# Attention, a rational layer and a routed layer on one core: softmax scaling, an affine step and a weight conversion recast

## The chip, the cores and the metric

The kernel runs on one core of a Trainium2 chip. The metric is the device time of one execution in microseconds; the median of three runs is given. A core has a matrix engine (PE, whose weight loads are listed as PEld), a vector engine (DVE), a scalar engine (ACT, or ScalarE), GpSimd (POOL) and a queue that starts transfers (SP).

## The reference

Three layers follow one another, on 4 x 576 = 2304 tokens of 512 features.

```python
# attention, 8 heads of 64, causal window of 128, ALiBi bias
scores = np.where(mask, scale * q @ k.T + bias, -1e9)
attn = np.exp(scores - scores.max(-1, keepdims=True))
attn = attn / (attn.sum(-1, keepdims=True) + 1e-9)
x = attn @ v
# rational layer, 512 -> 2048 -> 512
h = x @ w_in
P = a[0] + a[1]*h + a[2]*h**2 + a[3]*h**3
Q = 1 + abs(b[0])*abs(h) + abs(b[1])*h**2
y = (P / (Q + 1e-6)) @ w_out
# routed layer: 8 experts, 512 -> 1024 -> 512, one expert a token
e = argmax(y @ w_gate)
out = softmax(y @ w_gate)[e] * (relu(y @ w1[e]) @ w2[e])
```

The weights of the rational layer come as float64 numbers.

## The kernel before

**Stage A** takes the 2304 tokens in 9 chunks of 256. For each chunk it runs the rational layer in 8 steps; a step multiplies two 128-column slices of `w_in` (`up`, L366 to L368), turns the result `h_ps` into `P/Q` (`rational`, L380 to L415), and two steps later multiplies by the matching rows of `w_out` (`down`, L375 to L377). Each number is carried as two float32r parts, so that three products stand for one. Beside the steps of chunk c runs the attention of chunk c+1: four pairs of heads, one yield of `attention` for every second step. **Stage B** then runs the chosen experts in chunks of 256 tokens, with weights that are loaded and split on the way (`load_split`).

**Attention of a pair of heads.** A chunk of 256 tokens falls into two or three tiles of up to 128 rows, because 576 is no multiple of 256. For a tile and its two heads r = 0, 1: scores on PE (L290 or L299), bias and maximum on DVE (L304, with an accumulator read behind it), exponential and row sum on ACT (L309), 1e-9 added to the two sums (L313), reciprocal (L316), the division by the sum (L327 on DVE, in chunk 0 L325 on ACT, in chunk 1 L319 on POOL), the transposes on PE (L336), the copy to SBUF on ACT (L341, or L344 where the two blocks of keys differ in rows), and P.V on PE (L347), which writes head 0 to the output partitions 0 to 63 and head 1 to 64 to 127:

```python
for r in range(2):
    for i, (_, n, vb) in enumerate(blocks):
        nc.tensor.matmul(x_ps[D*r:D*r+D, qcol:qcol+L], v_sb[0:n, vb, D*r:D*r+D],
                         pt_sb[0:n, r, i, 0:L], start=(i == 0), stop=(i == nb - 1))
```

There are 80 such pairs of heads and tiles: 8 in chunk 0, 8 in chunk 1, 64 in chunks 2 to 8. In 16 of them one block of keys has 128 rows and the other 64. A float32 matmul stands in the trace as two instructions.

**Rational layer of a step** (tiles of 128 x 512): `ah` = |h| on ACT (L387), `u` = a3 h + a2 on ACT (L388), `qq` = |b1||h| + |b0| on DVE (L394; in chunk 0 on ACT, L390), `qq` times `ah` on POOL (L397), logarithm and exponential on ACT (L398, L399) for the reciprocal, five products on DVE (L400 to L410), the rounded part on ACT (L413) and the rest of it on POOL (L414).

**Conversion of the float64 weights** (`fetch64`, `magnitude64`, `split64`), in chunk 0: 16 tiles, each in two halves of 128 x 512. A half is one Abs on ACT (L170), four DVE instructions (clamp L171, shift L180, two steps that join bits, L183 and L186), one rounding on ACT (L189) and one subtraction on POOL (L190). The first 14 tiles (`EARLY`) lie whole in slots of the ring of weights and are handled as two views; the last two come as two tiles each.

**Order of the work.** The kernel is written with tiles; a scheduler that simulates the engines sets the order of each engine's instructions when the program is built (`schedule_with_timeline_sim=True`). On the chip each engine takes its instructions in that order.

Of the kernel before, what the change touches and what calls it, by code (L numbers as in the profile page):

```python
# [22 lines left out]
P = 128  # L23
T = 256
RING = 16               # resident weight tiles
RAWB = 2
EARLY = 14              # float64 tiles staged in the slots of the weights to come
AH1, AH2 = 2, 1         # how far the loads and the magnitudes run ahead of the splits
LEAD0, LEADR, LEAD = 0, 1, 4
PACK = 2                # from this chunk on, q and k are split into float32r parts  # L30
ACTN, POOLN = (0,), (1,)  # chunks whose softmax is divided by its sum on ScalarE, on GpSimd
QQA = (0,)              # chunks whose denominators start on ScalarE
POOLLO = (1, 4, 7)      # weight tiles of an expert whose lower parts GpSimd computes
JP, JT = 0, 1           # steps of a chunk at which the next one is gathered and transposed
JP0, JT0, JE = 2, 3, 2

# The upper words of the float64 numbers 2^-127 and of the greatest one below 2^128, read as float32.
# [5 lines left out]
def attention_rational_moe_kernel(  # L43
# [89 lines left out]

    yd = dram.tile([NT + 1, DM], F32, name="yd")
# [15 lines left out]
    def fetch64(f):  # L150
        src = wpack[f].bitcast(I32)
        if f < EARLY:
            raw = ring.tile([P, 2, DM, 2], I32, name="raw64", tag="ring")
            nc.sync.dma_start(out=raw.rearrange("p h n t -> p (h n t)"), in_=src)
            raws[f] = [raw[:, i] for i in range(2)]
# [7 lines left out]
    def magnitude64(f):  # L163
        if f < EARLY:
            a = ring.tile([P, 2, DM], F32, name="mag", tag="ring")
            mags[f] = [a[:, i] for i in range(2)]
        else:
            mags[f] = [ahp.tile([P, DM], F32, name="mag", tag="ah") for _ in range(2)]
        for i, (raw, a) in enumerate(zip(raws[f], mags[f])):
# [5 lines left out]
    def split64(f):  # L175
        w = ring.tile([P, 2, 2 * DM], F32R, name="w", tag="ring")
        for i, (raw, a) in enumerate(zip(raws.pop(f), mags.pop(f))):
            cs = slice(i * DM, (i + 1) * DM)
# [80 lines left out]
    def attention(c, xh, xl):  # L259
        for hp in range(H // 2):  # L260
# [6 lines left out]
            # Rows 0..63 and 64..127 hold both parts of q against the same part of k, so that two  # L267
            # products of the full height give all four terms of a head.
# [14 lines left out]
            for L, qcol, k0, wn, bo, blocks in tiles:  # L283
# [3 lines left out]
                su = sm.tile([P, 2], F32, name="su")  # L287
# [15 lines left out]
                for r in range(2):  # L303
# [7 lines left out]
                        bias=nm[0:L, r:r + 1], accum_out=su[0:L, r:r + 1],  # L311
                    )
                nc.vector.tensor_scalar(  # L313
                    out=su[0:L], in0=su[0:L], scalar1=1e-9, scalar2=None, op0=ALU.add
                )
                nc.vector.reciprocal(out=su[0:L], in_=su[0:L])  # L316
                for r in range(2):
                    if c in POOLN:
                        nc.gpsimd.tensor_scalar(  # L319
                            out=p_sb[0:L, r, 0:wn], in0=p_sb[0:L, r, 0:wn],  # L320
                            scalar1=su[0:L, r:r + 1], scalar2=None, op0=ALU.mult,
                        )
                        continue
                    if c in ACTN:
                        nc.scalar.mul(p_sb[0:L, r, 0:wn], p_sb[0:L, r, 0:wn], su[0:L, r:r + 1])  # L325
                        continue
                    nc.vector.tensor_scalar(  # L327
                        out=p_sb[0:L, r, 0:wn], in0=p_sb[0:L, r, 0:wn],
                        scalar1=su[0:L, r:r + 1], scalar2=None, op0=ALU.mult,
                    )  # L330
# [433 lines left out]
```

## Time and profile before

| | us |
|---|---|
| median of 3 runs (lowest, highest) | 960.73 (960.16, 961.38) |
| span of the profiled execution | 957.6 |
| PE busy | 857.6 (90%) |
| PEld busy | 731.5 (76%) |
| DVE busy | 762.1 (80%) |
| ACT busy | 573.2 (60%) |
| POOL busy | 507.1 (53%) |

The span runs from the first to the last instruction of the profiled execution; its whole time is not given apart, so the median of the runs, which lies 3.1 us above that span, stands for it. An engine's busy share is a mean over stages with different limits, and matmuls overlap in the profile, so that a busy PE is not PE at its peak. The start-to-start distance of two instructions on an engine tells more of what one costs than its duration.

### The profile page before, as it was taken

The page shows a single profiled execution, that of the slowest core. Times are in us where ns is not written, and L with a number is a line of the kernel's source. Part 1 is how long each engine was busy: PE and PEld are TensorE (multiplying, and loading weights), DVE is VectorE, ACT ScalarE, POOL GpSimd, SP SyncE. Part 2 cuts the span into 40 slices and gives each one's busy share as a digit, 9 for nine tenths or more (in the row PEclk, how much of TensorE's full clock was granted, in tenths as well). Part 3 has the DMA queues.
Part 4 walks back from the last instruction along what each step waited for, and adds up shares of the span by engine and source line. Part 5 has one row for each costly group of instructions (what it writes and reads, how often), then busy time and mean ns, then how long its engine had stood idle before and what let it go on. Part 6 is the DMA issues. An engine that isn't in the chain of part 4 may idle for free. (4 is left out here: it accounts for less than half of the span.)

```text
span 957.6 us, 16505 instructions
## 1 busy us (share of the span) xinstructions
PE 857.6 (90%) x5550; PEld 731.5 (76%) x5550; DVE 762.1 (80%) x1601; ACT 573.2 (60%) x1250; POOL 507.1 (53%) x433
## 2 busy tenths in 40 slices
PE   4557888998999899899899999999998989999994
PEld 2236577887988778778778778788778979999993
DVE  8999989897998998997998998969767875555510
ACT  5767676666676567666566676655536755555510
POOL 7457885453544554544444445435547855555500
PEclk9998899998999999999999999999999999999997
DMA  8553021022123122212112113000149976667400
GB/s 309 206 180 120 33 71 50 31 65 72 48 55 96 34 57 76 58 42 67 37 54 65 52 46 92 10 23 1 56 153 319 319 265 221 221 224 256 148 6 19
DMA packets 69962, 101.89 MB, mean 106 GB/s; under 512 B 14706, under 2 KB 47346, under 8 KB 68083
## 3 DMA queue, kind: packets, MB, share of 16 engines
q1 hardware_dynamic: 64658, 86.11, 28.0%
q0 software_dynamic: 5216, 14.70, 4.4%
q8 instruction: 45, 0.74, 0.3%
q14 instruction: 43, 0.34, 0.1%
HBM read 91.13 MB, written 10.17 MB: 106 GB/s over the span
## 5 line engine op out<-in xcount | busy, mean ns | idle before, releaser
L366 PE MATMUL h_ps<-x,w 128*128 128x256 f32 x896 | 263.9, 297 | 24.8 <-DVE u L401 10.9
L367 PE MATMUL h_ps<-x,w 128*128 128x256 f32 x896 | 262.5, 293 | 7.6 <-DVE x L354 4.2
L368 PE MATMUL h_ps<-x,w 128*128 128x256 f32 x896 | 261.5, 292 | 0.7 <-POOL w L210 0.5
L366 PEld LDWEIGHTS h_ps<-x,w 128*128 128x128 f32 x896 | 176.5, 198 | 36.1 <-issue 16.2
L367 PEld LDWEIGHTS h_ps<-x,w 128*128 128x128 f32 x896 | 177.3, 198 | 13.7 <-DVE x L354 5.3
L375 PE MATMUL y_ps<-w,gh 128*128 128x512 f32 x448 | 180.8, 404 | 3.9 <-ACT gh L413 2.7
L368 PEld LDWEIGHTS h_ps<-x,w 128*128 128x128 f32 x896 | 177.3, 198 | 2.7 <-POOL w L210 1.0
L376 PE MATMUL y_ps<-w,gh 128*128 128x512 f32 x448 | 178.8, 399 | 0.0
L377 PE MATMUL y_ps<-w,gl 128*128 128x512 f32 x448 | 169.5, 400 | 1.0 <-POOL gl L414 1.0
L397 POOL TENSOR_TENSOR qq<-qq,ah 128x512 f32<-128x512 f32 x72 | 98.8, 1373 | 102.1 <-DVE qq L394 78.6
L414 POOL TENSOR_TENSOR gl<-u,gh 128x512 fp32r<-128x512 f32 x72 | 98.7, 1372 | 98.1 <-ACT gh L413 73.5
L210 POOL TENSOR_TENSOR w<-rawh,w 128x512 fp32r<-128x512 f32 x60 | 87.8, 1484 | 49.1 <-ACT w L209 48.7
L309 ACT ACTIVATE p_sb<-p_sb,nm 128x256 f32<-128x256 f32 (+4 forms) x160 | 75.0, 470 | 52.1 <-DVE nm L304 49.3
L377 PEld LDWEIGHTS y_ps<-w,gl 128*128 128x128 f32 x448 | 85.2, 190 | 21.4 <-POOL gl L414 3.7
L375 PEld LDWEIGHTS y_ps<-w,gh 128*128 128x128 f32 x448 | 85.6, 191 | 20.6 <-ACT gh L413 4.5
L376 PEld LDWEIGHTS y_ps<-w,gh 128*128 128x128 f32 x448 | 85.8, 192 | 14.6 <-issue 0.3
L278 POOL TENSOR_TENSOR qk<-k_sb,qk 128x384 fp32r<-128x384 f32 (+1 forms) x56 | 63.7, 1145 | 46.4 <-ACT qk L274 37.7
L413 ACT CAST gh<-u 128x512 fp32r<-128x512 f32 x72 | 44.6, 619 | 54.9 <-DVE u L410 54.5
L347 PE MATMUL x_ps<-pt_sb,v_sb 128*64 128x128 f32 (+3 forms) x576 | 60.9, 294 | 10.6 <-ACT pt_sb L341 8.2
L190 POOL TENSOR_TENSOR w<-mag,w 128x512 fp32r<-128x512 f32 x32 | 51.7, 1632 | 30.3 <-ACT w L189 30.2
L398 ACT ACTIVATE r<-qq,qc 128x512 f32<-128x512 f32 x72 | 51.9, 722 | 26.2 <-POOL qq L397 26.2
L404 DVE SCALAR_TENSOR_TENSOR u<-u,co,r 128x512 f32<-128x512 f32 x72 | 59.3, 823 | 10.3 <-ACT r L399 10.2
(141 smaller groups left out, 1694.9 us busy)
## 6 DMA issues: line engine op xcount, KB each, us to landing
rawh<-epack SPq DMA_DIRECT2D x100, 256.0 KB, 5.3
raw<-epack SPq DMA_DIRECT2D x30, 512.0 KB, 5.6
raw<-wpack SPq DMA_DIRECT2D x14, 1024.0 KB, 7.1
v_sb<-vv SPq DMA_DIRECT2D x92, 64.0 KB, 2.0
k_sb<-kT SPq DMA_DIRECT2D x28, 192.0 KB, 3.6
q_sb<-qT SPq DMA_DIRECT2D x40, 128.0 KB, 2.8
yd<-y_sb POOLq DMA_DIRECT2D x18, 256.0 KB, 2.8
k_sb<-kT SPq DMA_DIRECT2D x16, 160.0 KB, 3.1
```

The source lines that it names most:

```text
L210: (nc.gpsimd if i in POOLLO else nc.vector).tensor_tensor(out=w[:, 1, cs], in0=raw, in1=w[:, 0, cs].bitcast(F32), op=ALU.subtract)
L278: nc.gpsimd.tensor_tensor(out=kl, in0=k_sb[:, r, 0:kc], in1=kh.bitcast(F32), op=ALU.subtract)
L309: nc.scalar.activation(out=p_sb[0:L, r, 0:wn], in_=p_sb[0:L, r, 0:wn], func=AF.Exp, scale=-1.0, bias=nm[0:L, r:r + 1], accum_out=su[0:L, r ...
L347: nc.tensor.matmul(x_ps[D * r:D * r + D, qcol:qcol + L], v_sb[0:n, vb, D * r:D * r + D], pt_sb[0:n, r, i, 0:L], start=(i == 0), stop=(i == ...
L366: nc.tensor.matmul(out_ps, w[:, 0, ws], xh[:, k, :], start=(k == 0), stop=False)
L367: nc.tensor.matmul(out_ps, w[:, 0, ws], xl[:, k, :], start=False, stop=False)
L368: nc.tensor.matmul(out_ps, w[:, 1, ws], xh[:, k, :], start=False, stop=(k == KD - 1))
L375: nc.tensor.matmul(y_ps[t], gh[:, i, ts], w[:, 0, DM:], start=a, stop=False)
L376: nc.tensor.matmul(y_ps[t], gh[:, i, ts], w[:, 1, DM:], start=False, stop=False)
L377: nc.tensor.matmul(y_ps[t], gl[:, i, ts], w[:, 0, DM:], start=False, stop=z)
L397: nc.gpsimd.tensor_tensor(out=qq, in0=qq, in1=ah, op=ALU.mult)
L414: nc.gpsimd.tensor_tensor(out=gl, in0=u, in1=gh.bitcast(F32), op=ALU.subtract)
```

## The change

Five edits. The affine step of every chunk goes to ACT. The sums of a pair lie in one of three constant tiles whose second column holds 1e-9, and one reduction over the two columns takes the place of the addition. Outside chunk 0 the division of both heads is one product of two tensors on DVE, in which the reciprocals are broadcast along the keys; POOL has no share in it any more. The first 14 float64 tiles are converted whole. In P.V the loop over blocks is the outer one.

```diff
+    sums = [const.tile([P, 2, 2], F32, name=f"sum{i}") for i in range(3)]
+    n_sums = [0]
+    for su in sums:
+        nc.vector.memset(su, 1e-9)
...
         if f < EARLY:
-            raw = ring.tile([P, 2, DM, 2], I32, name="raw64", tag="ring")
-            nc.sync.dma_start(out=raw.rearrange("p h n t -> p (h n t)"), in_=src)
-            raws[f] = [raw[:, i] for i in range(2)]
+            raw = ring.tile([P, 2 * DM, 2], I32, name="raw64", tag="ring")
+            nc.sync.dma_start(out=raw.rearrange("p n t -> p (n t)"), in_=src)
+            raws[f] = [raw]
...
         if f < EARLY:
-            a = ring.tile([P, 2, DM], F32, name="mag", tag="ring")
-            mags[f] = [a[:, i] for i in range(2)]
+            mags[f] = [ring.tile([P, 2 * DM], F32, name="mag", tag="ring")]
...
-                su = sm.tile([P, 2], F32, name="su")
+                su = sums[n_sums[0] % len(sums)]
+                n_sums[0] += 1
+                ri = sm.tile([P, 2], F32, name="ri")
...
-                        bias=nm[0:L, r:r + 1], accum_out=su[0:L, r:r + 1],
+                        bias=nm[0:L, r:r + 1], accum_out=su[0:L, r, 0:1],
                     )
-                nc.vector.tensor_scalar(
-                    out=su[0:L], in0=su[0:L], scalar1=1e-9, scalar2=None, op0=ALU.add
-                )
-                nc.vector.reciprocal(out=su[0:L], in_=su[0:L])
-                for r in range(2):
-                    if c in POOLN:
-                        nc.gpsimd.tensor_scalar(
-                            out=p_sb[0:L, r, 0:wn], in0=p_sb[0:L, r, 0:wn],
-                            scalar1=su[0:L, r:r + 1], scalar2=None, op0=ALU.mult,
-                        )
-                        continue
-                    if c in ACTN:
-                        nc.scalar.mul(p_sb[0:L, r, 0:wn], p_sb[0:L, r, 0:wn], su[0:L, r:r + 1])
-                        continue
-                    nc.vector.tensor_scalar(
-                        out=p_sb[0:L, r, 0:wn], in0=p_sb[0:L, r, 0:wn],
-                        scalar1=su[0:L, r:r + 1], scalar2=None, op0=ALU.mult,
+                nc.vector.tensor_reduce(out=ri[0:L], in_=su[0:L], op=ALU.add, axis=AX.X)
+                nc.vector.reciprocal(out=ri[0:L], in_=ri[0:L])
+                if c in ACTN:
+                    for r in range(2):
+                        nc.scalar.mul(p_sb[0:L, r, 0:wn], p_sb[0:L, r, 0:wn], ri[0:L, r:r + 1])
+                else:
+                    nc.vector.tensor_tensor(
+                        out=p_sb[0:L, :, 0:wn], in0=p_sb[0:L, :, 0:wn],
+                        in1=ri[0:L].unsqueeze(2).to_broadcast([L, 2, wn]), op=ALU.mult,
                     )
...
-                for r in range(2):
-                    for i, (_, n, vb) in enumerate(blocks):
+                for i, (_, n, vb) in enumerate(blocks):
+                    for r in range(2):
...
-        if c in QQA:
-            nc.scalar.activation(
-                out=qq, in_=ah, func=AF.Identity, scale=babs[:, 1:2], bias=babs[:, 0:1]
-            )
-        else:
-            nc.vector.tensor_scalar(
-                out=qq, in0=ah, scalar1=babs[:, 1:2], scalar2=babs[:, 0:1], op0=ALU.mult, op1=ALU.add
-            )
+        nc.scalar.activation(
+            out=qq, in_=ah, func=AF.Identity, scale=babs[:, 1:2], bias=babs[:, 0:1]
+        )
```

The scheduler sets the order anew on every engine. Three places follow.

DVE at the conversion of the first two weight tiles (`mag`, `raw`), before:

```order
L171 TENSOR_SCALAR mag<-mag 128x512
L180 TENSOR_SCALAR mag<-mag 128x512
L171 TENSOR_SCALAR mag<-mag 128x512
L183 SCALAR_TENSOR_TENSOR mag<-raw_286,mag 128x512
L180 TENSOR_SCALAR mag<-mag 128x512
L186 SCALAR_TENSOR_TENSOR mag<-raw_286,mag 128x512
L183 SCALAR_TENSOR_TENSOR mag<-raw_286,mag 128x512
L171 TENSOR_SCALAR mag<-mag 128x512 x2
L186 SCALAR_TENSOR_TENSOR mag<-raw_286,mag 128x512
```

and now:

```order
L175 TENSOR_SCALAR mag<-mag 128x1024
L186 TENSOR_SCALAR mag<-mag 128x1024
L189 SCALAR_TENSOR_TENSOR mag<-raw_292,mag 128x1024
L175 TENSOR_SCALAR mag<-mag 128x1024
L192 SCALAR_TENSOR_TENSOR mag<-raw_292,mag 128x1024
```

The four instructions of a tile stand once in place of twice, with twice the columns.

DVE in the middle of stage A, where the softmax of a pair (`su`, now `sum` and `ri`; `p_sb`) stands among the products of the rational layer (`u`, `qq`), before:

```order
L313 TENSOR_SCALAR su<-su 128x2
L354 TENSOR_TENSOR x<-x_ps,x 128x256
L401 SCALAR_TENSOR_TENSOR u<-u,co,h_ps 128x512
L316 RECIPROCAL su<-su 128x2
L327 TENSOR_SCALAR p_sb<-p_sb,su 128x256 x2
L404 SCALAR_TENSOR_TENSOR u<-u,co,r_4531 128x512
L407 SCALAR_TENSOR_TENSOR qq<-qq,qc,r_4531 128x512
L410 SCALAR_TENSOR_TENSOR u<-qq,u 128x512
L394 TENSOR_SCALAR qq<-ah,babs 128x512
```

and now:

```order
L321 TENSOR_REDUCE ri<-sum_189 128x2
L396 SCALAR_TENSOR_TENSOR u<-u,co,h_ps 128x512
L322 RECIPROCAL ri<-ri 128x2
L327 TENSOR_TENSOR p_sb<-p_sb,ri 128x512
L312 ISA p_sb,nm<-s_ps,bm 128x256
L312 ISA nm 128x1
L312 ISA p_sb,nm<-s_ps,bm 128x256
L312 ISA nm 128x1
L399 SCALAR_TENSOR_TENSOR u<-u,co,r_4532 128x512
```

Two products have become one, the addition a reduction, and the affine step has left DVE.

ACT at the same place, a step of the rational layer (`ah`, `u`, `qq`, `r`, `gh`), before:

```order
L387 ACTIVATE ah<-h_ps 128x512
L388 ACTIVATE u<-h_ps,co 128x512
L413 CAST gh<-u 128x512
L309 ACTIVATE p_sb,su<-p_sb,nm 128x256
L398 ACTIVATE r_4666<-qq,qc 128x512
L341 COPY pt_sb<-pt_ps 128x512
L399 ACTIVATE r_4666<-r_4666 128x512
```

and now:

```order
L388 ACTIVATE u<-h_ps,co 128x512
L317 ACTIVATE p_sb,sum_190<-p_sb,nm 128x256
L389 ACTIVATE qq<-ah,babs 128x512
L317 ACTIVATE p_sb,sum_190<-p_sb,nm 128x256
L341 COPY pt_sb<-pt_ps 128x512
L408 CAST gh<-u 128x512
L393 ACTIVATE r_4588<-qq,qc 128x512
```

The affine step stands in ACT's queue ahead of the copy of the transposed tile.

## Rows read from the trace of the kernel before

**Rows 1.** Busy time by stretch: PE, PEld, DVE, ACT, POOL, clock, DMA.

```profile
core 0: us, PE busy (x) PEld busy (x) DVE busy (x) ACT busy (x) POOL busy (x), PEclk, DMA share, GB/s
0.00:130.00 130.00, 84.32 (x417) 59.33 (x418) 125.67 (x275) 86.58 (x200) 90.48 (x103) 0.95 0.47 166
130.00:690.00 560.00, 527.07 (x3580) 450.86 (x3579) 494.70 (x1153) 359.82 (x848) 277.51 (x227) 0.98 0.19 51
```

**Rows 2.** PE's waits, 140 to 690 us: total us, times, longest.

```profile
PE pt_ps L336 <- DVE p_sb L327: 8.4, 12, 1.8
...
PE y_ps L375 <- ACT gh L413: 2.3, 3, 0.9
...
PE h_ps L366 <- DVE oh L461: 1.5, 2, 0.8
```

**Rows 3.** DVE groups by form, 0 to 130 us: count, busy us, mean ns, idle before.

```profile
L183 DVE SCALAR_TENSOR_TENSOR mag<-raw,mag 128x512 int32<-128x512 int32 x31 | 26.0, 856 | 0.0
L180 DVE TENSOR_SCALAR mag<-mag 128x512 int32<-128x512 int32 x31 | 24.3, 804 | 0.1
L186 DVE SCALAR_TENSOR_TENSOR mag<-raw,mag 128x512 int32<-128x512 int32 x31 | 23.4, 768 | 0.0
L171 DVE TENSOR_SCALAR mag<-mag 128x512 f32<-128x512 f32 x32 | 19.5, 626 | 1.2 <-ACT mag L170 1.2
```

**Rows 4.** DVE in order of time, 42 to 52 us: start us, length us.

```profile
42.95 1.28 DVE L183 SCALAR_TENSOR_TENSOR mag<-raw,mag 128x512 int32<-128x512 int32 x2
...
50.70 0.41 DVE L180 TENSOR_SCALAR mag<-mag 128x512 int32<-128x512 int32 x1
51.03 0.68 DVE L183 SCALAR_TENSOR_TENSOR mag<-raw,mag 128x512 int32<-128x512 int32 x1
```

**Rows 5.** POOL groups, 0 to 130 us: the scaling of chunk 1.

```profile
L319 POOL TENSOR_SCALAR p_sb<-p_sb,su 128x256 f32<-128x256 f32 x15 | 20.9, 1402 | 4.7 <-DVE su L316 4.7
```

**Rows 6.** Single lines: count, shortest/median/longest ns, first and last start.

```profile
L480 DVE TENSOR_REDUCE se<-lg x9: 142/157/170, 183.5 to 707.4; 128x2 f32<-128x16 f32 x9
...
L327 DVE TENSOR_SCALAR p_sb<-p_sb,su x128: 237/347/2066, 150.5 to 634.6; 128x256 f32<-128x256 f32 x72, 64x192 f32<-64x192 f32 x24, 128x128 f32<-128x128 f32 x16, 64x64 f32<-64x64 f32 x8
...
L390 ACT ACTIVATE qq<-ah,babs x8: 810/814/824, 79.8 to 145.4; 128x512 f32<-128x512 f32 x8
```

**Rows 7.** All groups of the span that the change removes from DVE.

```profile
L327 DVE TENSOR_SCALAR p_sb<-p_sb,su 128x256 f32<-128x256 f32 (+3 forms) x128 | 65.2, 549 | 1.2
...
L394 DVE TENSOR_SCALAR qq<-ah,babs 128x512 f32<-128x512 f32 x64 | 44.1, 688 | 23.1 <-ACT ah L387 23.0
...
L313 DVE TENSOR_SCALAR su<-su 128x2 f32<-128x2 f32 (+1 forms) x80 | 29.7, 371 | 3.9 <-ACT p_sb L309 3.4
```

**Rows 8.** DVE groups by form, 130 to 690 us.

```profile
L410 DVE SCALAR_TENSOR_TENSOR u<-qq,u 128x512 f32<-128x512 f32 x67 | 54.4, 813 | 0.7
...
L327 DVE TENSOR_SCALAR p_sb<-p_sb,su 128x256 f32<-128x256 f32 x72 | 41.3, 614 | 0.7
```

**Rows 9.** PE in order of time, 438 to 443 us: P.V of three tiles.

```profile
438.31 0.67 PE L347 MATMUL x_ps<-pt_sb,v_sb 128*64 128x128 f32 x8
438.90 0.39 PE L367 MATMUL h_ps<-x,w 128*128 128x256 f32 x1
...
440.29 1.10 PE L347 MATMUL x_ps<-pt_sb,v_sb 128*64 128x64 f32 x8
441.31 0.30 PE L336 MATMUL pt_ps<-ident,p_sb 64*64 64x64 f32 x2
...
442.21 0.33 PE L347 MATMUL x_ps<-pt_sb,v_sb 64*64 64x64 f32 x4
442.47 0.66 PE L439 MATMUL pt_ps<-ident,y_sb 128*128 128x128 f32 x4
```

**Rows 10.** PE in order of time, 510 to 512 us: P.V of a fourth.

```profile
510.62 1.51 PE L347 MATMUL x_ps<-pt_sb,v_sb 64*64 64x128 f32 x8
512.06 0.55 PE L336 MATMUL pt_ps<-ident,p_sb 128*128 128x128 f32 x3
```

More of the change, by code (lines that the diff above doesn't have):

```diff
@@ L30 @@
 PACK = 2
-ACTN, POOLN = (0,), (1,)
-QQA = (0,)
+ACTN = (0,)
 POOLLO = (1, 4, 7)
@@ L164, in magnitude64 @@
         if f < EARLY:
-            a = ring.tile([P, 2, DM], F32, name="mag", tag="ring")
-            mags[f] = [a[:, i] for i in range(2)]
+            mags[f] = [ring.tile([P, 2 * DM], F32, name="mag", tag="ring")]
         else:
             mags[f] = [ahp.tile([P, DM], F32, name="mag", tag="ah") for _ in range(2)]
-        for i, (raw, a) in enumerate(zip(raws[f], mags[f])):
+        for raw, a in zip(raws[f], mags[f]):
             nc.scalar.activation(out=a, in_=raw.bitcast(F32)[:, :, 1], func=AF.Abs)
@@ L176, in split64 @@
         w = ring.tile([P, 2, 2 * DM], F32R, name="w", tag="ring")
-        for i, (raw, a) in enumerate(zip(raws.pop(f), mags.pop(f))):
-            cs = slice(i * DM, (i + 1) * DM)
+        parts = list(zip(raws.pop(f), mags.pop(f)))
+        for i, (raw, a) in enumerate(parts):
+            n = 2 * DM // len(parts)
+            cs = slice(i * n, (i + 1) * n)
             ai = a.bitcast(I32)
@@ L377, in down, with rational @@
                 nc.tensor.matmul(y_ps[t], gl[:, i, ts], w[:, 0, DM:], start=False, stop=z)
-    def rational(h_ps, c):
+    def rational(h_ps):
         u = ep.tile([P, 2, T], F32, name="u")
@@ L698, in attention_rational_moe_kernel @@
                 flush()
-            g = rational(h_ps, c)
+            g = rational(h_ps)
             pend.append((j, NF1 // 2, partial(route, c), w_res[2 * j:2 * j + 2], *g))
```

## The prediction

> **What bounds the kernel now.** I read the busy time by stretch first [rows 1]. In the first 130 us DVE is busy 125.7 us and PE 84.3: this is chunk 0, in which the float64 weights are converted, and DVE is the limit. From 130 to 690 us, the rest of stage A, PE is busy 527.1 of 560 us (94%), DVE 494.7 (88%), ACT 359.8 (64%), POOL 277.5. PE is the limit there, but DVE runs so close behind it that PE has to wait for it. PE's own waits say how much [rows 2]: seven rows name DVE, from 8.4 us for the scaled softmax tile down to 1.5 us, 20.7 us in all; the largest that names ACT is 2.3. Stage B, from 690 us, holds none of the edits and is costed at nothing: what covers it is that its weights and products stay as they are.
>
> So a microsecond taken from DVE counts almost in full before 130 us, and afterwards only as far as PE waits for DVE. One taken from PE counts almost in full between 130 and 690 us.
>
> **1. Conversion of 14 tiles whole (chunk 0).** DVE's four instructions on two halves become four on a whole, 56 instructions fewer. Undisturbed, one join of 512 columns takes 0.68 us, and two in a row 1.28, so that the next starts 0.08 us before the end [rows 4]. What a second instruction costs beside its columns isn't shown; the reduction of 16 columns, at 0.157 us [rows 6], bounds it from above, and nothing bounds it from below. With the 0.08 overlap taken off it is 0.08, and 56 x 0.08 = 4.5 us; I take 4, ends 0 and 56 x 0.157 = 8.8. ACT and POOL save as many starts, 28 and 14, beside DVE's work. A first product that had needed only half a tile now waits for a whole; DVE is the limit for the tiles behind it, so I cost that at nothing, and at 2.7 us if it isn't covered, the four instructions on the other half of one tile (0.86 + 0.80 + 0.77 + 0.63 = 3.1 us at their means [rows 3], less 0.4 saved).
>
> **2. 1e-9 by a reduction.** The addition takes 29.7 us in 80 instructions, 371 ns each [rows 7]; a reduction of 16 columns to 2 takes 157 [rows 6], and the new one has 4. 80 x 0.214 = 17.1 us: 3.4 in the first 130 us, 13.7 after. Three fills of 4 columns come on top, under 0.5 us. The reductions seen run 142 to 170 ns, never longer.
>
> **3. One product for both heads.** Chunk 1 first. Its 16 scalings leave POOL, 20.9 us [rows 5] of the 90.5 us that POOL is busy before 130 us [rows 1], and 8 products come to DVE. DVE pays for POOL: the four conversion steps take 856, 804, 768 and 626 ns on the mean [rows 3] against 0.68 and 0.41 us undisturbed [rows 4], together 31 x (0.176 + 0.394 + 0.088) + 32 x 0.216 = 27.3 us of waiting. With 20.9/90.5 of POOL's time gone I take off 6.3 us, ends 0 and twice that. The 8 products have 512 columns and two tensors, like the join, whose mean in this stretch is 0.86 us: + 6.9, ends 5.4 (at 0.68) and 6.9. Chunks 2 to 8: 128 scalings take 65.2 us [rows 7], 72 of them with 256 columns 41.3 [rows 8], and 36 products take their place. A product of two tensors of 512 columns takes 54.4/67 = 0.81 us there [rows 8]: 36 x 0.81 = 29.2, 12.1 less, and at the same ratio 7.0 less for the other 56: 19 us. At undisturbed lengths there would be no gain, 2 x 0.347 [rows 6] against 0.68 [rows 4]; that is the lower end. I take 19, since a scaling waits twice for a pair where the product waits once. The Trainium skill speaks against this edit (VectorE: DVE Perf Modes, "The perf-mode tier table"): float32 `tensor_scalar` on SBUF runs at 2x, `tensor_tensor` at 1x. The undisturbed rows agree with it, 0.35 us for 256 columns and 0.68 for 512; by it alone DVE would keep these 19 us, and the time would come out 2 us higher.
>
> **4. |b1||h| + |b0| on ACT.** DVE loses 44.1 us in 64 instructions [rows 7], ACT gains 64 x 0.814 = 52 us [rows 6].
>
> **DVE after 130 us**: 13.7 + 19 + 44.1 = 77 us less, 494.7 becomes 418 (75%), its idle time goes from 65 to 142 us. PE's waits of 20.7 us should fall with the time DVE is free; in proportion they would be 9.5. Ends: nothing gained, 20.7 gained. I take 10.
>
> **ACT after 130 us**: 360 becomes 412 us (74%). Its price on PE isn't shown. Bounds: nothing, and 52 us if every added step stood bare before a matmul. DVE, at 88%, costs PE 20.7/494.7 = 4% of its busy time, and 52 x 4% is 2; since the step stands ahead of copies that PE needs, I take 3. The product on POOL waits for its input anyway, and the two steps between `rational` and `down` cover 0.3 us more before it.
>
> **5. Heads alternate in P.V.** Where all blocks have equal rows, 8 instructions on 64 columns each cost 0.59 us to the next matmul (438.31 to 438.90) [rows 9]: the heads already run side by side, since 8 weights and 8 streams of 128 columns one after another would be longer, as the next row shows. Where one block has 128 rows and one 64, 8 instructions with half the columns cost 1.02 us (440.29 to 441.31), while one block for both heads costs 0.26 (442.21 to 442.47) [rows 9]. So a change of rows between two blocks is what forces the heads apart. With heads inside and blocks outside each block should cost what it costs alone: 2 x 0.26 in place of 1.02, 0.50 us saved, in 12 tiles. Four more have 128 columns and cost 1.44 us (510.62 to 512.06) [rows 10]; between 0.59 and 2 x 0.37 (half of 0.59 with 0.07 for the change, an estimate) I take 0.70, 0.74 saved. 12 x 0.50 + 4 x 0.74 = 9 us of PE, times PE's 94%: 8.5. The other 64 pairs gain nothing. The Trainium skill has the rule (TensorEngine Tiling (Array Packing), "Key Properties"): tiles run independently, and a change of tiling mode drains the engine. By it only these 16 pairs gain; without it, if only neighbours in the order could run side by side, all would, and the trace's 0.59 us speaks for the rule.
>
> **Sum.** First 130 us: - 4 - 3.4 - 6.3 + 6.9 = - 7. After: - 10 (DVE) + 3 (ACT) - 8.5 (P.V). Together - 22.5 us. The profiled span is 957.6 us, 3.1 below the median of the runs, 960.7, and I carry these 3.1 over: 935.1 + 3.1 = 938 us.
>
> **Rivals.**
> *DVE's relief stays on DVE.* The scheduler orders everything anew, and PE's waits may come from the length of a chain and not from DVE's load. For it: the largest row is 12 waits for the scaled tile [rows 2], and one product of two heads ends later than the first of two scalings. Against it: at 88% a queue is more often late than at 75%. Then 960.7 - 7 - 8.5 + 3 = 948.
> *P.V gains nothing*, because the engine doesn't take up the order it is given: 938 + 8.5 = 946.5. Against it: the one-block group at 0.26 us.
> *ACT turns into the late engine: slower.* The affine step stands in ACT's queue ahead of the copy of the transposed tile, and while PE waits for that copy it does nothing else that is ready. Each time it stands bare it costs 0.814 us. The other terms save 25.5 us, so it decides from 31 of 64 steps on; with 44 of 64 it costs 36, and the time is 971. For it: ACT is the engine that gains load, and it is served in order. Against it: 26% idle is left, more than DVE has now, and chunk 0 ran with the step on ACT already.
> *Chunk 0 gets longer*, with DVE the limit and 6.9 us of products added there, and neither POOL's time nor starts saved: + 3.5 in place of - 7, 948.
>
> **How the numbers follow.** The forecast, 930 to 946, has 0.55; relief that stays on DVE 0.14, no gain in P.V 0.07, a longer chunk 0 0.08, ACT late 0.09; 0.04 is left for losses that cancel the gains, within 0.2% of 960.7, which is about what a measurement of this kernel can tell from no change, and 0.03 for still more than 930. That makes faster 0.87, same 0.04, slower 0.09. From 927 to 955 the range holds all but the slow cases, the even one and a part of the tails.
>
> **What would show it.** Right: DVE near 75% between 130 and 690 us, ACT near 74%; no wait on the added reduction over 0.2 us; the 16 mixed groups of P.V at 0.5 to 0.7 us; PE reaching 94% some 7 us sooner; PE's waits for DVE near 10 us. Wrong: PE waiting for the copies of transposed tiles by 10 us or more; mixed groups still over 1 us; chunk 0 ending later; the new product over 1 us on the mean.

## The result, and the profile after

The changed kernel takes **933.45 us** (median of 5 runs, 932.49 to 939.27) against 960.73 for the kernel before (5 runs, 959.77 to 963.29): ratio 0.972 with its 95% interval from 0.969 to 0.974, 27.3 us faster. Forecast were 938 us and 927 to 955.

The profiled execution of the changed kernel is the longest of its five, 939.27 us with a span of 937.5; the other four spans run from 930.8 to 933.4. So the two traces differ by 957.6 - 937.5 = 20.1 us where the medians differ by 27.3. The granted clock of TensorE, as a mean over the execution, is also the lowest of the five in this one, 0.962 against 0.971 to 0.980; that the clock is the cause is not shown. Where the 20.1 us went, the traces tell.

The page of the changed kernel, busy time of each engine in the span:

```profile
PE 846.0 (90%) x5550; PEld 727.4 (78%) x5550; DVE 729.0 (78%) x1428; ACT 610.9 (65%) x1286; POOL 486.5 (52%) x403
```

Busy time by stretch, columns as in [rows 1]:

```profile
0.00:130.00 130.00, 78.81 (x382) 54.95 (x383) 124.75 (x224) 81.39 (x166) 63.07 (x74) 0.89 0.48 166
130.00:690.00 560.00, 536.37 (x3720) 464.05 (x3719) 474.09 (x1060) 413.72 (x934) 291.82 (x233) 0.98 0.20 57
```

POOL has given up 27 us of the first 130 (90.48 to 63.07), and DVE is busy there as long as before (125.67, now 124.75): chunk 0 did not get shorter. To compare the same work, a mark in the program serves better than a clock time. Step `oh` of the ranking runs once a chunk; its line in each kernel, with shortest, median and longest ns, and the first and the last start:

```profile
L461 DVE TENSOR_TENSOR oh<-pick,pm x9: 159/175/1261, 182.0 to 707.2; 128x16 bf16<-128x16 f32 x9
```

```profile
L456 DVE TENSOR_TENSOR oh<-pick,pm x9: 166/174/934, 181.2 to 688.5; 128x16 bf16<-128x16 f32 x9
```

Up to the first mark the change gives 0.8 us. Between first and last mark, 525.2 us become 507.3: 17.9 us. From the last mark to the end, 250.4 become 249.0. The stretches between the marks, the kernel before first, then the changed one:

```profile
182.00:707.00 525.00, 495.05 (x3380) 423.39 (x3379) 461.08 (x1080) 335.00 (x787) 254.89 (x210) 0.99 0.20 56
```

```profile
181.00:688.00 507.00, 486.14 (x3389) 420.85 (x3387) 427.07 (x964) 376.36 (x856) 261.71 (x211) 0.98 0.21 58
```

PE is busy 8.9 us less, and idle 20.9 us in place of 30.0, 9.1 less: these two make the 18. DVE is busy 34 us less, but its share falls only from 88% to 84%. PE's waits in the changed kernel, 140 to 690 us, which answer to [rows 2]:

```profile
PE pt_ps L336 <- DVE p_sb L327: 6.4, 6, 3.2
...
PE h_ps L366 <- DVE u L396: 2.6, 5, 0.9
PE s_ps L307 <- DVE qk L281: 2.4, 3, 1.0
PE h_ps L366 <- ACT x L353: 1.9, 2, 1.1
...
PE x_ps L347 <- ACT pt_sb L341: 0.3, 1, 0.3
```

The seven largest rows that name DVE add up to 16.2 us, where the seven of the kernel before made 20.7. No wait for a copied tile (`pt_sb`) is over 0.3 us: ACT did not become the late engine.

P.V in the order of time on PE, in the changed kernel, which answers to [rows 9] and [rows 10]:

```profile
431.90 0.60 PE L347 MATMUL x_ps<-pt_sb,v_sb 128*64 128x64 f32 x8
432.43 0.30 PE L336 MATMUL pt_ps<-ident,p_sb 64*64 64x64 f32 x2
...
496.42 0.80 PE L347 MATMUL x_ps<-pt_sb,v_sb 64*64 64x128 f32 x8
497.16 0.39 PE L367 MATMUL h_ps<-x,w 128*128 128x256 f32 x1
```

The group of 64 columns now costs 0.53 us to the next matmul in place of 1.02, the one of 128 columns 0.74 in place of 1.44.

Last, groups of DVE over the whole span, and among them the added step on ACT; they answer to [rows 7]:

```profile
L399 DVE SCALAR_TENSOR_TENSOR u<-u,co,r 128x512 f32<-128x512 f32 x72 | 64.8, 901 | 13.3 <-ACT r L394 12.8
L405 DVE SCALAR_TENSOR_TENSOR u<-qq,u 128x512 f32<-128x512 f32 x72 | 64.5, 896 | 0.8
L327 DVE TENSOR_TENSOR p_sb<-p_sb,ri 128x512 f32<-128x512 f32 (+4 forms) x72 | 64.4, 894 | 1.4
L389 ACT ACTIVATE qq<-ah,babs 128x512 f32<-128x512 f32 x72 | 58.6, 814 | 0.0
...
L321 DVE TENSOR_REDUCE ri<-sum 128x2 f32<-128x4 f32 (+1 forms) x80 | 11.8, 148 | 12.1 <-ACT p_sb L317 11.7
```

The first two belong to the rational layer, and no edit touches them. In the kernel before they are L404 and L410:

```profile
L404 DVE SCALAR_TENSOR_TENSOR u<-u,co,r 128x512 f32<-128x512 f32 x72 | 59.3, 823 | 10.3 <-ACT r L399 10.2
L410 DVE SCALAR_TENSOR_TENSOR u<-qq,u 128x512 f32<-128x512 f32 x72 | 58.1, 808 | 0.7
```

They grew by 5.5 and 6.4 us. That is the first sign of what the experiments came to: work taken from DVE came back there in part, in other instructions.

### The profile page after: what moved, and what is told of

It is laid out like the page before. It is cut to its first block, busy times and chain, and to the rows that moved or that the text cites. A ratio compares the mean times of both kernels' runs of the same rounds, so it can differ in the third digit from the quotient of the medians.

```text
span 937.5 us, 16318 instructions
## 1 busy us (share of the span) xinstructions
PE 846.0 (90%) x5550; PEld 727.4 (78%) x5550; DVE 729.0 (78%) x1428; ACT 610.9 (65%) x1286; POOL 486.5 (52%) x403
## 3 DMA queue, kind: packets, MB, share of 16 engines
q1 hardware_dynamic: 64658, 86.11, 28.9%
## 5 line engine op out<-in xcount | busy, mean ns | idle before, releaser
L409 POOL TENSOR_TENSOR gl<-u,gh 128x512 fp32r<-128x512 f32 x72 | 102.0, 1417 | 104.1 <-ACT gh L408 79.2
L392 POOL TENSOR_TENSOR qq<-qq,ah 128x512 f32<-128x512 f32 x72 | 101.2, 1405 | 96.1 <-ACT qq L389 93.0
L399 DVE SCALAR_TENSOR_TENSOR u<-u,co,r 128x512 f32<-128x512 f32 x72 | 64.8, 901 | 13.3 <-ACT r L394 12.8
L196 POOL TENSOR_TENSOR w<-mag,w 128x1024 fp32r<-128x1024 f32 (+1 forms) x18 | 44.8, 2489 | 51.6 <-ACT w L195 51.6
L395 DVE TENSOR_TENSOR u<-u,h_ps 128x512 f32<-128x512 f32 x72 | 48.9, 679 | 28.5 <-ACT u L388 28.3
L216 DVE TENSOR_TENSOR w<-raw,w 128x1024 fp32r<-128x1024 f32 x30 | 49.4, 1646 | 25.7 <-ACT w L215 25.6
```

Of the source, the lines that this page charges most:

```text
L216: (nc.gpsimd if i in POOLLO else nc.vector).tensor_tensor(out=w[:, 1, cs], in0=raw, in1=w[:, 0, cs].bitcast(F32), op=ALU.subtract)
L392: nc.gpsimd.tensor_tensor(out=qq, in0=qq, in1=ah, op=ALU.mult)
L399: nc.vector.scalar_tensor_tensor(out=u, in0=u, scalar=co[:, 0:1], in1=r0, op0=ALU.add, op1=ALU.mult)
L409: nc.gpsimd.tensor_tensor(out=gl, in0=u, in1=gh.bitcast(F32), op=ALU.subtract)
```

## The experiments

All ratios are against the kernel before on the same chip, whose medians were 959.5, 959.5 and 959.9 us in the three sets. "After" means the changed kernel with one thing edited, "before" the old one. The changed kernel itself was not run again in these sets, so that a difference from its 933.45 us goes across sets. The kernel before spreads from 949.6 to 964.3 us over its 64 runs of the three sets, with granted clocks from 0.982 to 0.966: a difference of a few us between two kernels is no finding by itself.

### The conversion, and POOL's instruction

**u_halves**: after, with the 14 tiles converted in halves again.

```diff
-            raw = ring.tile([P, 2 * DM, 2], I32, name="raw64", tag="ring")
...
-            raws[f] = [raw]
+            raw = ring.tile([P, 2, DM, 2], I32, name="raw64", tag="ring")
...
+            raws[f] = [raw[:, i] for i in range(2)]
...
-            mags[f] = [ring.tile([P, 2 * DM], F32, name="mag", tag="ring")]
+            a = ring.tile([P, 2, DM], F32, name="mag", tag="ring")
+            mags[f] = [a[:, i] for i in range(2)]
```

> The changed kernel with one edit undone: the first 14 float64 tiles are converted in halves again. Theory A (a whole tile makes POOL's subtraction 2.5 us long, and DVE's steps wait for it as long as the saved starts were worth): no difference, 931 to 936 us against 933.5. Theory B (the forecast's term, 4 us of saved starts in a stretch where DVE is the limit): 937 to 941 us. Theory C (whole tiles cost more than they save): 926 to 930 us.

936.46 us (932.95 to 936.6, 4 runs), 0.978 [0.973, 0.982]: as the changed kernel within the intervals. The first mark lies at 182.9 us, against 181.2. This edit brings nothing in time that these runs can measure.

The run also separates the start costs from the waiting, since in it and in the kernel before the conversion has the same instructions. Busy time up to 181 us (PE, PEld, DVE, ACT, POOL), the kernel before first, then u_halves:

```profile
0.00:181.00 181.00, 130.94 (x708) 98.87 (x709) 168.30 (x356) 118.83 (x270) 121.63 (x126) 0.94 0.38 132
```

```profile
0.00:181.00 181.00, 127.31 (x697) 96.20 (x698) 172.15 (x352) 118.89 (x267) 99.78 (x109) 0.93 0.39 132
```

POOL is busy 21.9 us less, and yet DVE's four steps of the conversion take 99.2 us in place of 96.3.

**poolhalf**: after, with POOL's subtraction of a tile in two instructions of 512 columns, so that whole tiles no longer make POOL's instruction longer.

```diff
-            nc.gpsimd.tensor_tensor(
-                out=w[:, 1, cs], in0=a, in1=w[:, 0, cs].bitcast(F32), op=ALU.subtract
-            )
+            for k in range(n // DM):
+                ks = slice(i * n + k * DM, i * n + (k + 1) * DM)
+                nc.gpsimd.tensor_tensor(
+                    out=w[:, 1, ks], in0=a[:, k * DM:(k + 1) * DM],
+                    in1=w[:, 0, ks].bitcast(F32), op=ALU.subtract,
+                )
```

> The changed kernel, whole tiles on ACT and DVE, but POOL's subtraction of a tile in two instructions of 512 columns. Theory A: a DVE step never waits longer than 1.3 us for POOL, the joins' mean falls from 1.7 to about 1.4 us, and the time by 3 to 6 us, to 927 to 931. Theory B (length of POOL's instruction doesn't matter): 932 to 936 us, joins unchanged.

935.32 us (933.54 to 936.7, 4 runs), 0.977 [0.973, 0.981], first mark at 180.9 us: the same again. DVE's groups of the conversion in the changed kernel, 0 to 181 us by form, and the product of chunk 1 (the four rows of the last two tiles are left out):

```profile
L189 DVE SCALAR_TENSOR_TENSOR mag<-raw,mag 128x1024 int32<-128x1024 int32 x14 | 24.9, 1781 | 0.2
L192 DVE SCALAR_TENSOR_TENSOR mag<-raw,mag 128x1024 int32<-128x1024 int32 x14 | 24.3, 1736 | 0.0
L175 DVE TENSOR_SCALAR mag<-mag 128x1024 f32<-128x1024 f32 x14 | 14.9, 1063 | 0.7 <-ACT mag L174 0.7
L186 DVE TENSOR_SCALAR mag<-mag 128x1024 int32<-128x1024 int32 x14 | 14.5, 1035 | 0.1
...
L327 DVE TENSOR_TENSOR p_sb<-p_sb,ri 128x512 f32<-128x512 f32 x8 | 8.4, 1052 | 0.0
```

With the last two tiles the conversion takes 93.9 us of DVE, 89.7 with POOL's halves, and 99.2 in u_halves; the kernel before had 96.3 over its first 181 us. A join of a whole tile takes 1.21 us at the shortest of the trace, and 1.78 and 1.74 on the mean of its two steps. So the whole tiles save DVE 5.3 us (99.2 to 93.9), and POOL's smaller load in this stretch did not free the conversion. Nor does the length of POOL's instruction decide the time: with it halved DVE is busy 168.4 us up to 181 us, with it whole 170.0, and the time stays.

### One part undone

These four take one edit back from the changed kernel.

**u_affine**: |b1||h| + |b0| on DVE again, outside chunk 0.

```diff
+QQA = (0,)
...
-        nc.scalar.activation(
-            out=qq, in_=ah, func=AF.Identity, scale=babs[:, 1:2], bias=babs[:, 0:1]
-        )
+        if c in QQA:
+            nc.scalar.activation(
+                out=qq, in_=ah, func=AF.Identity, scale=babs[:, 1:2], bias=babs[:, 0:1]
+            )
+        else:
+            nc.vector.tensor_scalar(
+                out=qq, in0=ah, scalar1=babs[:, 1:2], scalar2=babs[:, 0:1], op0=ALU.mult, op1=ALU.add
+            )
...
```

> The changed kernel with |b1||h|+|b0| back on DVE outside chunk 0. Theory A (PE waits less because DVE has idle time): 44 us back on DVE between 130 and 690 us, DVE near 92% busy there, time 941 to 947 us. Rival (relief stays on DVE): 932 to 936 us. If ACT had become the late engine, it would be faster: under 931.

943.86 us (941.22 to 945.65, 4 runs), 0.987 [0.983, 0.991]: 10.4 us over the changed kernel.

**u_product**: two products with a number for each row again, one for each head, on DVE in chunk 1 too.

```diff
-                    nc.vector.tensor_tensor(
-                        out=p_sb[0:L, :, 0:wn], in0=p_sb[0:L, :, 0:wn],
-                        in1=ri[0:L].unsqueeze(2).to_broadcast([L, 2, wn]), op=ALU.mult,
-                    )
+                    for r in range(2):
+                        nc.vector.tensor_scalar(
+                            out=p_sb[0:L, r, 0:wn], in0=p_sb[0:L, r, 0:wn],
+                            scalar1=ri[0:L, r:r + 1], scalar2=None, op0=ALU.mult,
+                        )
```

> The changed kernel with two scalings on DVE for the two heads in place of one product, in chunk 1 too. Forecast's term: 19 us more DVE time after 130 us and a little in chunk 0, of which PE sees an eighth to a quarter: 936 to 939 us. Rival (undisturbed lengths are equal, so nothing changes): 931 to 935 us.

951.78 us (949.95 to 955.15, 11 runs), 0.994 [0.991, 0.998]: 18.3 us over the changed kernel. Its group on DVE, to be held against L327 above (64.4 us in 72):

```profile
L328 DVE TENSOR_SCALAR p_sb<-p_sb,ri 128x256 f32<-128x256 f32 (+4 forms) x144 | 82.8, 615 | 1.5
```

**u_eps**: 1e-9 added by an instruction of its own again.

```diff
-                nc.vector.tensor_reduce(out=ri[0:L], in_=su[0:L], op=ALU.add, axis=AX.X)
+                nc.vector.tensor_scalar(
+                    out=ri[0:L], in0=su[0:L, :, 0], scalar1=1e-9, scalar2=None, op0=ALU.add
+                )
```

> The changed kernel with 1e-9 added by a tensor_scalar on the two sums. Forecast's term: the instruction waits for POOL again, 0.2 us more on the mean, 14 us of DVE after 130 us and 3 before: 935 to 940 us. Rival (such a small wait falls into DVE's idle time): 931 to 935 us, with the addition's mean near 0.37 us all the same.

962.01 us (959.22 to 963.88, 11 runs), 1.004 [1.001, 1.007]: 28.6 us over the changed kernel, and so the whole gain, for 80 instructions on two columns.

**u_heads**: P.V head by head again.

```diff
-                for i, (_, n, vb) in enumerate(blocks):
-                    for r in range(2):
+                for r in range(2):
+                    for i, (_, n, vb) in enumerate(blocks):
```

> The changed kernel with P.V head by head again. Theory A (only a change of rows between two blocks forces the heads apart, 16 pairs): each mixed group takes 0.5 to 0.7 us more, 9 us of PE in all, time 940 to 943 us; the 64 other pairs keep 0.59 us. Rival (order of heads is free, gain came from elsewhere): 932 to 936 us, mixed groups still 0.5 us.

949.9 us (947.43 to 951.88, 7 runs), 0.991 [0.988, 0.994]: 16.5 us over the changed kernel.

What follows is first of all a puzzle. Undone one at a time, the parts cost 3.0 + 10.4 + 18.3 + 28.6 + 16.5 = 76.8 us, where the whole change is worth 27.3. The last three lie above every range that I had expected of them. Parts that can stand in for each other would give less than the whole when undone alone, not nearly three times as much; parts that work only together could give more, and the sum by itself doesn't exclude that. The scheduler orders everything anew for each edit, so I tried what an order alone is worth.

### The same work in another order

**flip**: after, with the two heads of P.V taken in the order 1, 0. The instructions and their sizes are the same.

```diff
-                    for r in range(2):
+                    for r in (1, 0):
```

> The changed kernel with the two heads of a block in P.V in the other order (1, 0). The work of every engine is the same to the instruction, only the scheduler's order differs in thousands of places: this measures how far the time moves by a new order alone. Theory A (the 7 us by which undoing the head order cost more than its 9 us of PE came from the new order): flip lies 3 to 8 us away from 933.5. Rival (alternation saves 16 us by itself, order moves the time by less than 2 us): 931 to 936 us.

**946.27 us** (943.88 to 947.68, 5 runs), 0.989 [0.983, 0.994]: 12.8 us over the changed kernel with the same work, and the two sets of runs don't touch. The granted clock is not what parts them: from 0.971 to 0.976 three runs of flip take 943.9 to 946.8 us, and two of the changed kernel, at 0.971 and 0.973, 935.1 and 932.5. PE is busy no longer. The page and PE's waits from 140 to 690 us of flip:

```profile
PE 844.0 (90%) x5550; PEld 722.7 (77%) x5550; DVE 736.3 (78%) x1428; ACT 610.3 (65%) x1286; POOL 486.5 (52%) x403
```

```profile
PE y_ps L375 <- ACT gh L408: 9.4, 10, 2.5
PE pt_ps L336 <- DVE p_sb L327: 6.2, 4, 3.2
```

The second row stands nearly as in the changed kernel (6.4). The first is new: `down` waits 9.4 us for the cast of P/Q, which costs 0.2 us in the changed kernel. In the order of the two traces, line and buffer numbers left out, some 2,300 of the 8,667 instructions of PE, DVE, ACT and POOL stand elsewhere. Between the marks of flip (184.3 and 694.2 us):

```profile
184.00:694.00 510.00, 481.15 (x3357) 413.08 (x3356) 430.27 (x962) 373.00 (x847) 260.06 (x210) 0.99 0.21 58
```

PE is idle 510.0 - 481.15 = 28.9 us there, against 20.9 in the changed kernel: 8.0 us more, where the medians differ by 12.8. The two traces differ by 4.7 us in all; the changed kernel's is its longest run, and in it PE is busy 5.0 us longer between the marks, at a clock of 0.98 in place of 0.99.

**b_flip**: the same swap in the kernel before.

```diff
-                for r in range(2):
+                for r in (1, 0):
```

> The kernel before with the two heads of P.V in the other order (1, 0), blocks inside as before: the same work, a new order. Theory A (a new order moves either kernel by some 12 us, and the kernel before stood at its level by chance too): 945 to 975 us, more than 3 us from 960. Rival (only the changed kernel's order was a lucky one, the kernel before is stable): 957 to 963 us.

958.09 us (955.75 to 962.73, 11 runs), 1.001 [0.998, 1.004]: no change by the medians. The order is worth 12.8 us in the one kernel, and nothing that the medians show in the other. The granted clock is not alike here, though: of the runs at 0.976 and over, ten of b_flip take 955.8 to 962.7 us and seven of the kernel before 951.4 to 956.2, so a few us of order may be hidden behind the clock.

**mixed_only**: after, alternating only in the 16 groups in which the rows of the blocks differ; the other 64 go head by head.

```diff
+                steps = [(i, r) for i in range(nb) for r in range(2)]
+                if all(n == blocks[0][1] for _, n, _ in blocks):
+                    steps.sort(key=lambda s: s[1])
+                for i, r in steps:
+                    _, n, vb = blocks[i]
...
```

> The changed kernel with heads alternating only in the 16 pairs whose blocks differ in rows, head by head in the 64 others. Theory A (only the 16 gain, 9 us): within what a new order moves, 931 to 938 us, uniform groups still 0.59 us. Rival (the 64 gain as well, some 7 us): 939 to 942 us.

944.28 us (943.36 to 949.64, 5 runs), 0.988 [0.982, 0.994]. A group with equal rows costs the same either way, 594 and 587 ns to the next matmul, so this kernel has the changed kernel's work too, and it lies 10.8 us above it. Between its marks (179.8 and 694.0 us) PE is idle 28.4 us, as in flip:

```profile
180.00:694.00 514.00, 485.63 (x3387) 418.62 (x3385) 434.45 (x965) 376.42 (x856) 263.51 (x211) 0.98 0.21 57
```

What makes the run useful is that its order is u_heads' on DVE, ACT and POOL throughout, and on PE in all but 34 of 5,550 instructions: the two differ in the 16 groups alone. The group of P.V over the span, in u_heads and then in mixed_only:

```profile
L347 PE MATMUL x_ps<-pt_sb,v_sb 128*64 128x128 f32 (+3 forms) x576 | 62.5, 296 | 10.4 <-ACT pt_sb L341 7.6 <-ACT w L195 2.7
```

```profile
L350 PE MATMUL x_ps<-pt_sb,v_sb 128*64 128x128 f32 (+2 forms) x576 | 53.5, 296 | 10.8 <-ACT pt_sb L341 7.9 <-ACT w L195 2.7
```

One mixed tile at the same place on PE's timeline, again u_heads first:

```profile
430.32 1.10 PE L347 MATMUL x_ps<-pt_sb,v_sb 128*64 128x64 f32 x8
```

```profile
430.52 0.60 PE L350 MATMUL x_ps<-pt_sb,v_sb 128*64 128x64 f32 x8
```

9.0 us of PE less, and 5.6 us of time by the medians, 2.7 by the ratios. Their intervals overlap, so that the time saved is not shown beyond the noise, and its size is known to no better than that. PE's idle time between the marks rises from 24.8 to 28.4 us, so that a part of what P.V. gives back is waited off.

u_halves and poolhalf belong beside these two. Their orders depart from the changed kernel's as well, on PE in 362 and 405 of 5,550 instructions (flip 1,357, mixed_only 875), and their times agree with its within the intervals, with PE idle 18.7 and 21.2 us between their marks. So not every new order loses.

**eps_flip**: flip, with the 1e-9 added by an instruction of its own.

```diff
-                nc.vector.tensor_reduce(out=ri[0:L], in_=su[0:L], op=ALU.add, axis=AX.X)
+                nc.vector.tensor_scalar(
+                    out=ri[0:L], in0=su[0:L, :, 0], scalar1=1e-9, scalar2=None, op0=ALU.add
+                )
...
-                    for r in range(2):
+                    for r in (1, 0):
```

> The changed kernel with 1e-9 added by a tensor_scalar, as in the run that undid this edit, and the two heads of P.V in the other order. Theory A (the addition itself costs, because it waits for POOL in the middle of the softmax chain): 955 to 965 us again. Rival (its 28 us came from the new order): 937 to 950 us, near the run that only swapped the heads.

954.78 us (952.54 to 957.41, 11 runs), 0.996 [0.993, 0.999]. In the traces its order is flip's in all but 2 of the 8,667 instructions, the additions themselves aside. So the addition costs 8.5 us by the medians, 6.9 by the ratios, and the 28.6 us of u_eps held some 20 us that the order brought. PE's wait for the scaled tile, 6.2 us in flip, is 11.1 here. The page of eps_flip, and then its group of the addition:

```profile
PE 848.9 (89%) x5550; PEld 726.9 (76%) x5550; DVE 746.5 (78%) x1428; ACT 610.9 (64%) x1286; POOL 485.7 (51%) x403
```

```profile
L321 DVE TENSOR_SCALAR ri<-sum 128x2 f32<-128x2 f32 (+1 forms) x80 | 34.4, 429 | 10.6 <-ACT p_sb L317 10.1
```

Against the reduction's 11.8 us in flip the line grows by 22.6 us, but DVE as a whole only by 746.5 - 736.3 = 10.2. What these instructions wait for the trace shows best at the longest of them. DVE and POOL in u_eps, in order of time:

```profile
465.97 1.00 POOL L493 DMA_INDIRECT tab<-val,slot  x1 [0.30 <-issue]
466.60 5.36 DVE L321 TENSOR_SCALAR ri<-sum 128x2 f32<-128x2 f32 x1 [0.76 <-ACT p_sb L317]
467.00 1.28 POOL L411 TENSOR_TENSOR gl<-u,gh 128x512 fp32r<-128x512 f32 x1
468.23 1.26 POOL L394 TENSOR_TENSOR qq<-qq,ah 128x512 f32<-128x512 f32 x1
469.45 1.26 POOL L411 TENSOR_TENSOR gl<-u,gh 128x512 fp32r<-128x512 f32 x1
470.67 1.25 POOL L394 TENSOR_TENSOR qq<-qq,ah 128x512 f32<-128x512 f32 x1
```

POOL is issuing an indirect transfer when the addition begins; its four products follow without a gap and end at 470.67 + 1.25 = 471.92 us; the addition of two columns, begun at 466.60, ends at 471.96, after all four of them. The same in the changed kernel, DVE and POOL around 309 us:

```profile
308.60 1.02 POOL L284 TENSOR_TENSOR qk<-k_sb,qk 128x384 fp32r<-128x384 f32 x1 [1.12 <-ACT qk L280]
...
308.69 0.15 DVE L321 TENSOR_REDUCE ri<-sum 128x2 f32<-128x4 f32 x1
...
308.96 0.69 DVE L453 TENSOR_TENSOR pick<-lg,mx 128x16 f32<-128x16 f32 x1
...
309.58 1.30 POOL L409 TENSOR_TENSOR gl<-u,gh 128x512 fp32r<-128x512 f32 x1
309.68 1.22 DVE L454 TENSOR_TENSOR pick<-pick,desc 128x16 f32<-128x16 f32 x1
```

The reduction runs through beside POOL's instruction. The two products of 16 columns behind it end with POOL's, at 309.65 (POOL: 309.62) and 310.90 (310.88). The Trainium skill (SBUF — State Buffer, "Who interferes with whom") has this as a rule: DVE shares a pair of ports with GpSimd, a reduction on trn2 never needs it, an operation with two inputs in SBUF needs it beside a GpSimd instruction that reads SBUF, a `tensor_scalar` in its two-port mode needs it too, and whoever comes second waits for the whole instruction of the other. The traces agree: 80 reductions take 130 to 159 ns, and of 80 additions in u_eps half take up to 163 ns and the longest 5,355.

### Parts on the kernel before

**a_affine**: before, with the affine step on ACT in all chunks.

```diff
-QQA = (0,)
+QQA = tuple(range(9))
```

> The kernel before with one of the five edits: |b1||h|+|b0| on ScalarE in all chunks, 44 us off DVE. Rival (DVE's load is what PE waits for): 948 to 954 us. Theory A (the affine step isn't in the chain that PE waits for): within what a new order moves, 955 to 968 us, with PE's waits for the scaled tile still at 8 us or more.

950.67 us (948.65 to 954.04, 11 runs), 0.992 [0.989, 0.995], 9.2 us below the 959.9 of the kernel before in this set, and about what u_affine lost (10.4). DVE falls to 728.8 us from 762.1, 33 for 44.1 us of instructions removed. PE's idle time between the marks falls from 30.0 to 25.0 us, but its wait for the scaled tile did not fall with it; a row of its waits, 140 to 690 us, beside the 8.4 of [rows 2]:

```profile
PE pt_ps L336 <- DVE p_sb L327: 14.2, 15, 2.1
```

**b_softmax**: before, with the reduction and the single product, chunk 1 on DVE.

```diff
...
-                nc.vector.tensor_scalar(
-                    out=su[0:L], in0=su[0:L], scalar1=1e-9, scalar2=None, op0=ALU.add
-                )
+                nc.vector.tensor_reduce(out=ri[0:L], in_=su[0:L], op=ALU.add, axis=AX.X)
...
-                    if c in POOLN:
-                        nc.gpsimd.tensor_scalar(
...
+                    nc.vector.tensor_tensor(
+                        out=p_sb[0:L, :, 0:wn], in0=p_sb[0:L, :, 0:wn],
+                        in1=ri[0:L].unsqueeze(2).to_broadcast([L, 2, wn]), op=ALU.mult,
+                    )
```

> The kernel before with two of the five edits: 1e-9 by the reduction, and one product for both heads (chunk 1 included). Theory A (PE waits for the softmax chain, which stands in PE's order ahead of other matmuls; these two edits carry the part of the gain that isn't P.V's): 940 to 950 us, PE's waits for the scaled tile below 7 us. Rival (DVE's load counts, of which these edits take 33 of 77 us): 953 to 957 us.

960.39 us (958.62 to 963.17, 11 runs), 1.004 [1.001, 1.007]: no gain. By my terms these two edits were to take 29 us off DVE (3.4 + 13.7 + 19 - 6.9); it falls by 2.4, from 762.1 to 759.7:

```profile
PE 858.2 (90%) x5550; PEld 736.2 (77%) x5550; DVE 759.7 (79%) x1548; ACT 575.4 (60%) x1250; POOL 493.1 (52%) x417
```

So the softmax edits alone don't carry the gain, whatever u_eps and u_product seem to say. In its trace two things stand against each other. Between the marks of b_softmax (183.6 and 706.9 us):

```profile
184.00:707.00 523.00, 499.25 (x3390) 430.29 (x3388) 454.83 (x1025) 339.01 (x794) 260.08 (x211) 0.97 0.21 56
```

PE is idle 23.8 us in place of 30.0, so the edits did spare it waits; but it is busy 4.2 us longer, at a granted clock of 0.97 in place of 0.99, and the first mark comes 1.6 us later. All eleven runs lie at 0.957 to 0.965, below each of the 33 runs of the kernel before in this set (0.967 to 0.980). Why the clock was lower no run shows.

## Why the prediction held, and which of its steps failed

The time came out 4.5 us below the forecast and inside the range. The mechanism of the sum, less load on PE and on DVE while ACT has room, is what the trace shows. Three of its terms were of the wrong size, and what made up for them is no term of mine: that the sum came out so near is luck in part.

- **Conversion and chunk 0 (forecast -7; measured -0.8 to the first mark).** The failed step is "with 20.9/90.5 of POOL's time gone I take off 6.3 us" of waiting. POOL lost more than that, and the conversion waited as long: 2.4 us less on its four steps, with the first term in it (4 us forecast; 5.3 us of DVE from u_halves to the changed kernel). Without the whole tiles, in u_halves, the steps take 2.9 us more than before. The addition gave 4.3 us up to 181 us (7.1 to 2.8), and the products took 7.7 (11.6 with the first of chunk 2, where 3.9 stood): the eight of chunk 1 cost 1.05 us each and not 0.86. That is 1.0 us more; DVE as a whole is busy 1.7 us longer there, 168.3 to 170.0. Of my rivals the fourth, "chunk 0 gets longer", comes nearest: POOL's time was not saved, though the starts were, and where it priced +3.5 us the mark came 0.8 us sooner.
- **1e-9 by a reduction (forecast 17.1 us of DVE).** 29.7 to 11.8, 17.9. None of the 80 reductions lasts over 159 ns, as said. With the order held nearly equal it is worth 6.9 to 8.5 us of time.
- **One product for both heads (forecast 19 us of DVE after chunk 1).** Mis-sized: the line goes from 65.2 us to 64.4 - 8.4 = 56.0, about 9. I had priced 512 columns at 0.81 us, from [rows 8], and they took 0.91 (33.8 us in 37, 130 to 690 us): the product has two inputs in SBUF, and I take it that with fewer other instructions to wait in, more of POOL's time fell on it. No run gives its worth in time with the order held.
- **The affine step on ACT (forecast 44.1 us off DVE, 52 onto ACT).** 814 ns each, as forecast, and ACT between 130 and 690 us at 413.7 us, 74%, as forecast. Two runs give 9.2 and 10.4 us for it, each across a change of order.
- **DVE's relief (forecast 75% busy, 10 us).** The failed step is the subtraction, "494.7 becomes 418 (75%)". Over the span the instructions removed come to 44.1 + 17.9 + 0.8 (product) + 2.4 (conversion) = 65 us, and DVE fell by 33. Half came back as longer instructions elsewhere, in L399, L405 and in `pick` of the ranking (2.6 to 7.6 us) 17 of it. Between the marks DVE is at 84%, and its seven largest rows still cost PE 16.2 us, where about 10 were forecast. All of PE's idle time there fell by 9.1 us, against 10 - 3 forecast for DVE and ACT together.
- **Heads alternate in P.V (forecast 9 us of PE, 8.5 of time).** The groups cost 0.53 and 0.74 us (forecast 0.52 and 0.70), PE is busy 8.9 us less between the marks, and 9.0 less from u_heads to mixed_only. In time 2.7 to 5.6 us at nearly the same order, with intervals that overlap. The 64 groups of equal rows gain nothing, as forecast (594 and 587 ns).
- **ACT late, the slower rival**: not seen. **Relief that stays on DVE**: true by half.

What no step held is the order. Three kernels do the changed kernel's work: it takes 933.5, 944.3 and 946.3 us in three orders that the scheduler made of nearly the same text. As far as these two slower orders stand for others, some 11 to 13 of the 27.3 us belong to a fortunate order, and some 15 to the edits; that split is an estimate from two orders, and u_halves and poolhalf show two more that keep the time. With the heads as 1, 0 on both sides the ladder is 958.1 (before), 954.8 (all but the reduction), 946.3 (all): 11.8 us. That the fortunate order is not itself the work of one of the edits can't be excluded; in the traces it shows as idle time of PE, 20.9 us against 28.9 in flip and 28.4 in mixed_only. Against flip the row that grew is the wait for the cast (9.2 us); against mixed_only the waits are spread over many rows, and what makes the order fortunate stays open. No kernel tried was faster than the changed one.

## What to carry to other kernels

Where a scheduler orders the whole program, undoing one part measures the part and a new order together: look for two kernels whose orders agree in nearly all rows, and take the price from those, or swap something that costs nothing and see how far the time moves. An instruction that waits for another engine is not worth its whole length when it is removed: here the line gave up 22.6 us and DVE as a whole 10.2, with the order kept, so that other instructions waited in its place. Compare the granted clock of the runs as well, before a change is called worth nothing. And a group of small matmuls on two halves of the array is worth ordering by rows: here that halved its time on PE.

## What was not expected of the hardware

- What DVE waits beside POOL moves between DVE's instructions. `u<-u,h_ps` (one input in PSUM) takes 678 to 680 ns on the mean in the changed kernel and in all others whose group was read, and `u<-u,co,h_ps` 740 to 742, while `u<-u,co,r`, of the same size and with its inputs in SBUF, ranges from 801 (u_affine) to 940 (u_heads).
- Two heads side by side on PE don't need to alternate as long as their blocks have equal rows: 587 ns for eight matmuls alternating, 594 head by head.
- A new order with the same instructions moved one kernel by 12.8 us, 1.4%, and the other by nothing that its medians show.
